# A two-layer kernel whose second layer takes its 256-token plain block first, between the last slots of layer one, with a scheduler that looks ahead

## The chip, the cores and the metric

The kernel runs on one core of one Trainium2 chip. The metric is the device time of one execution in microseconds (us). Each version is run several times; the median is compared.

## The reference

Windowed attention over q, k, v of 4 x 8 heads x 576 positions x 64 (half of the heads with a plain window of 32, half with a window of 32 at a stride of 4) gives x, 2304 tokens by 512. Two MLP layers follow:

```python
x = attention(q, k, v)              # 2304 x 512, float32
h = x @ moe_w_in                    # 512 x 2048
x = maximum(0.01 * h, h) @ moe_w_out
h = x @ moe2_w_in
out = (maximum(h, 0) + log1p(exp(-abs(h)))) @ moe2_w_out
```

All is float32. Matrix products take each operand as a high part in the matmul's own format and a low remainder, and add three products (high x high, high x low, low x high).

## The kernel before, in words

No order is written by hand. Every piece of work is an `Op` with an engine, a planned cost, dependencies, buffers that it takes (`acq`) and gives back (`rel`), and a due time (`target`, less `margin`). `run_schedule` (L109) plans all engines forward in time: an engine that is free takes the ready op with the earliest due time. The result is a list, and the instructions are emitted in that order; on the chip each engine then runs its own list strictly in order and waits where an operand isn't there. TensorE's list is fixed for the two layers by `chain`: each op of it is ordered behind the one before.

**Layer one** works in slots (`order`, L730). A slot is one block of tokens (256 to 352, mostly 288) with one of 16 pieces `f` of the hidden width. `g1` (L754, matmuls L747) makes a hidden tile in a PSUM bank `h`; ScalarE applies the leaky unit (`g1_leaky`, L763) and takes the high part (`g1_hi`, L768), VectorE the low part (`g1_lo`, L772); two slots later (`LAG`) `g2` (matmuls L790) adds it into the four banks `yp` of the block. After a block's last slot the four banks go through `y_evac` (ScalarE for e = 0 and 2, L798, VectorE for e = 1 and 3, L800) into `ys` (three buffers in SBUF), and `y_store` (L803) writes them to DRAM; a `ys` buffer is free again when its store has landed. The banks are then used by the next block, or, after the last block, by layer two. Attention for later blocks (scores L594, PV L674) and the conversion of the second layer's weights lie between the slots. The conversion loads a raw piece, and ScalarE's `rebias` (L282) is its first step; `C2A` and `C2B` set when pieces are due.

**Layer two** takes 2304 tokens as four blocks of 512 and one of 256 (`TL2`). For a block of 512, step m = (block c, pair of hidden pieces i) makes seven products of a 2 x 2 block scheme (`prod`, L924) of combined weights A11, A12, A22, S1 to S4 with combined inputs (`t_sum`, `t_hi`, `t_lo`), which VectorE adds into two units of 128 x 512. A unit passes |h|, exp, ln, 1+ (ScalarE, L959 to L970), three VectorE steps (L973 to L982), the high part on ScalarE (`hi`, L987) and the low part on VectorE (`lo`, L991); its |h| to `lo` holds one of the same three `ys` buffers. Then `g4` (L1014) multiplies it, in chunks of three matmuls, with `w_out` into four banks `yo`; at a block's end `o_evac` (L1022, L1024) copies each bank in two halves into one of five `o` buffers and `o_store` writes it out. `PATTERN` gives the order of products (digits) and chunks (a, b) in a step. The block of 256 tokens comes last: `plain` (L1002) makes its hidden tile `hp` directly, with A11, A12, A21, A22, and A21 is loaded late (`a21_load`) into S2's room. The second layer's weights (`comb_load`, L825; split by `comb_hi` L829 and `comb_lo` L833) use the rooms of layer one's weights as its last block frees them.

The change touches `run_schedule`, `comb_load` and its companions, `load_y`, `x_last`, `prod`'s numbering, `plain`, `o_store`, the constants, `pe`, `x_ready`, `product` and the loop that writes layer two's chain.

Of the kernel before, what the change touches and what calls it, by code (L numbers as in the profile page):

```python
# [11 lines left out]
F32 = mybir.dt.float32  # L12
# [14 lines left out]
def kernel(  # L27
# [80 lines left out]
    def run_schedule(slots):  # L108
# [53 lines left out]

        result = []
# [4 lines left out]
        while True:  # L168
# [14 lines left out]
            for e in engines:  # L183
# [10 lines left out]
                if e == "pe" and not opened and not best.optional and now - ready_at[best] < 0.3:  # L194

                    for o in pools[e]:
                        if o.optional and ready_at[o] <= now + 1e-9 and all(free[a] >= o.acq.count(a) for a in o.acq):
# [3 lines left out]
                            break  # L201
                pools[e].remove(best)
                for a in best.acq:
                    free[a] -= 1
# [14 lines left out]
                heapq.heappush(events, best.end)  # L219
                for u in best.next:  # L220
                    done(u, best.end if u.eng == e else now)
# [27 lines left out]
    class Piece:  # L249
# [52 lines left out]
        def sums(self, k):  # L302

            a = self.ct.bitcast(F32).rearrange("p (a n) -> p a n", a=4)
            if k == 0:
                self.cs = wraw.tile([P, 4, 2 * P], F32, tag="cp", name="cs", bufs=1)
            s = self.cs
            x, y, op = ((a[:, 2], a[:, 3], ALU.add), (s[:, 0], a[:, 0], ALU.subtract),
                        (a[:, 0], a[:, 2], ALU.subtract), (a[:, 1], s[:, 1], ALU.subtract))[k]
            nc.vector.tensor_tensor(out=s[:, k], in0=x, in1=y, op=op)  # L310
# [504 lines left out]
    def comb_load(i, half, j):  # L815
        if j == 0:
            comb[i, half] = wpool.tile([P, 4, 2, 2 * P], F32R, tag=f"w{2 * i + half}", name="w2")
            for n, nm in enumerate((("A11", "A12", "A22", "S1"), ("S2", "S3", "S4"))[half]):
                comb[i, nm] = comb[i, half][:, n]
            if half:  # L820
                spare[i] = comb[i, 1][:, 3].rearrange("p t n -> p (t n)")
        t = comb[i, half].bitcast(F32)
        dst, src = (((t[:, 0:2, 1], w2_a[i][:, 0:2]), (t[:, 2, 1], w2_a[i][:, 3]), (t[:, 3, 1], w2_s[i][:, 0])),
                    ((t[:, 0:3, 1], w2_s[i][:, 1:4]),))[half][j]
        nc.sync.dma_start(out=dst, in_=src)  # L825

    def comb_hi(i, half, j):
        t = comb[i, half][:, 2 * j:min(2 * j + 2, 4 - half)]
        nc.scalar.activation(out=t[:, :, 0], in_=t[:, :, 1].bitcast(F32), func=AF.Copy)  # L829

    def comb_lo(i, half, j):
        t = comb[i, half][:, 2 * j:min(2 * j + 2, 4 - half)]
        nc.vector.tensor_sub(out=t[:, :, 1], in0=t[:, :, 1].bitcast(F32), in1=t[:, :, 0].bitcast(F32))  # L833

    def a21_load(i):
        comb[i, "A21"] = comb[i, "S2"]
        nc.sync.dma_start(out=comb[i, "A21"][:, 1].bitcast(F32), in_=w2_a[i][:, 2])

    def a21_hi(i):
        t = comb[i, "A21"]  # L840
# [685 lines left out]
```

## Time and profile before

| | us |
|---|---|
| three runs | 925.34, 927.38, 930.04; median 927.38 |
| the profiled execution | 924.97 |
| its span, first to last instruction | 923.2 |
| TensorE (PE) busy | 886.5 (96%) |
| VectorE (DVE) busy | 707.4 (77%) |
| ScalarE (ACT) busy | 508.0 (55%) |
| GpSimd (POOL) busy | 136.7 (15%) |
| mean granted TensorE clock | 0.989 |

Layer one's matmuls fill the span to about 530 us, layer two's the rest; its block of 256 tokens runs from 865 us. An engine's idle time is told with what ended it. TensorE's number of matmuls is the same in both versions, so its idle time and its time at a granted clock below 1.00 are the parts to look at.

### The profile page before, as it was taken

To read this page: it belongs to the slowest core of one execution; us is meant where nothing else is said; L and a number is where in the kernel's file an instruction comes from. 1 tells how busy PE (TensorE), PEld (TensorE's weight loads), DVE (VectorE), ACT (ScalarE), POOL (GpSimd) and SP (SyncE) were. 2 spreads that over 40 slices of the span, in tenths; PEclk is the share of its full clock that TensorE was granted. 3 is DMA by queue.
4 is the path that set the end of the run, shared out by engine and by line. 5 is a ranking of instruction groups with operands and counts; after the bars stand their busy time and mean duration, and the time that the engine had idled before them with its cause. 6 is when DMAs were issued, how large, how long until landed. Compare 5 with 4: busy or idle time off the path is not lost.

```text
span 923.2 us, 16583 instructions
## 1 busy us (share of the span) xinstructions
PE 886.5 (96%) x6375; PEld 827.2 (90%) x6376; DVE 707.4 (77%) x1265; ACT 508.0 (55%) x983; POOL 136.7 (15%) x73
## 2 busy tenths in 40 slices
PE   6889999999999999999999979999999999999998
PEld 4779999999999999999999968888888888888887
DVE  3989994376796997978966777797778778777745
ACT  3768853334344434444456655675575666656554
POOL 4500030010352452423600000000000000000000
PEclk9979999999999999999999979999999999999999
DMA  8878122254555455554347823244335323533274
GB/s 228 212 226 293 21 43 48 75 139 141 166 127 182 109 145 162 157 148 126 125 154 228 311 88 92 92 142 151 104 107 171 103 93 122 169 118 113 98 224 164
DMA packets 157331, 131.90 MB, mean 143 GB/s; under 512 B 102340, under 2 KB 138180, under 8 KB 157124
## 3 DMA queue, kind: packets, MB, share of 16 engines
q1 hardware_dynamic: 154852, 130.26, 47.3%
q8 instruction: 50, 0.82, 0.4%
q10 hardware_dynamic: 2400, 0.59, 0.3%
q14 instruction: 29, 0.24, 0.1%
HBM read 104.60 MB, written 26.21 MB: 142 GB/s over the span
## 4 chain that ended last, share of the span: by engine, by line
PE 68%; DVE 14%; DMA 7%; ACT 3%; issue 2%; POOL 2%; SPq 1%; DVEq 0%; ACTq 0%; POOLq 0%
PE yo L1014 19%; PE h L747 15%; PE yp L790 15%; PE h L924 14%; PE hp L1002 2%; POOL sm L682 2%; DMA out_dram<-o 2%; DMA raw<-in_moe_w_out_dram 2%; PE sc L594 2%; DVE cf L300 2%; DMA yr<-y 1%; PE pv L643 1%; DMA y<-ys 1%; DVE xn L690 1%; SPq L487 1%
## 5 line engine op out<-in xcount | busy, mean ns | idle before, releaser
L1014 PE MATMUL yo<-wo,w 128*128 128x512 f32 x864 | 228.4, 399 | 10.6 <-ACT w L987 6.1
L747 PE MATMUL h<-xh,w 128*128 128x288 f32 (+2 forms) x1024 | 231.5, 301 | 1.2 <-DVE w L342 1.1
L790 PE MATMUL yp<-gh,w 128*128 128x288 f32 (+2 forms) x1024 | 229.2, 299 | 3.1 <-ACT ys L798 1.8
L1014 PEld LDWEIGHTS yo<-wo,w 128*128 128x128 f32 x864 | 153.2, 190 | 41.7 <-ACT w L987 6.5
L924 PEld LDWEIGHTS h<-tr,w 128*128 128x128 f32 x1344 | 175.0, 188 | 10.9
L924 PE MATMUL h<-tr,w 128*128 128x256 f32 x1344 | 177.4, 280 | 0.0
L790 PEld LDWEIGHTS yp<-gh,w 128*128 128x128 f32 x1024 | 171.6, 188 | 4.8 <-DVE ys L800 2.2
L747 PEld LDWEIGHTS h<-xh,w 128*128 128x128 f32 x1024 | 172.9, 190 | 2.8 <-DVE w L342 1.6
L747 PE MATMUL h<-xl,w 128*128 128x288 f32 (+2 forms) x512 | 152.1, 297 | 0.3 <-DVE xl L725 0.3
L790 PE MATMUL yp<-gl,w 128*128 128x288 f32 (+2 forms) x512 | 150.9, 295 | 0.0
L763 ACT ACTIVATE hc<-h 128x288 f32<-128x288 f32 (+2 forms) x128 | 52.1, 407 | 111.2 <-PE h L747 106.3
L747 PEld LDWEIGHTS h<-xl,w 128*128 128x128 f32 x512 | 97.3, 190 | 0.5 <-DVE xl L725 0.5
L790 PEld LDWEIGHTS yp<-gl,w 128*128 128x128 f32 x512 | 96.2, 188 | 0.4 <-DVE gl L772 0.3
L987 ACT ACTIVATE w<-ex 128x512 fp32r<-128x512 f32 (+1 forms) x73 | 45.4, 622 | 86.8 <-DVE ex L982 86.6
L618 POOL PARTITION_ALL_REDUCE mx<-s x24 | 50.2, 2090 | 265.6 <-DVE s L608 242.0
L772 DVE TENSOR_TENSOR gl<-hc,gh 128x288 fp32r<-128x288 f32 (+2 forms) x128 | 66.5, 521 | 26.5 <-ACT gh L768 25.9
L973 DVE SCALAR_TENSOR_TENSOR ln<-z,ln 128x512 f32<-128x512 f32 (+1 forms) x73 | 49.8, 683 | 40.8 <-ACT z L970 40.8
L282 ACT ACTIVATE cf<-raw 128x512 f32<-128x512 f32 (+1 forms) x48 | 39.9, 830 | 50.7 <-DMA raw<-in_moe_w_in_dram 26.5
L682 POOL PARTITION_ALL_REDUCE sm<-s x16 | 61.0, 3815 | 37.9 <-ACT s L625 37.9
L768 ACT ACTIVATE gh<-hc 128x288 fp32r<-128x288 f32 (+2 forms) x128 | 56.8, 444 | 3.1 <-ACT w L829 0.2
L991 DVE TENSOR_TENSOR w<-ex,w 128x512 fp32r<-128x512 f32 (+1 forms) x73 | 49.6, 679 | 9.6 <-ACT w L987 9.5
L300 DVE CUSTOM_DVE_ANT_0 cf<-raw,cf 128x1024 uint16<-128x1024 uint16 (+1 forms) x48 | 53.5, 1115 | 1.4
(108 smaller groups left out, 1164.7 us busy)
## 6 DMA issues: line engine op xcount, KB each, us to landing
wo<-w2o SPq DMA_DIRECT2D x80, 512.0 KB
raw<-in_moe_w_in_dram SPq DMA_DIRECT2D x32, 512.0 KB
raw<-in_moe_w_out_dram SPq DMA_DIRECT2D x32, 512.0 KB
w2o<-cf SPq DMA_DIRECT2D x16, 512.0 KB
out_dram<-o SPq DMA_DIRECT2D x36, 128.0 KB
w2a<-cf SPq DMA_DIRECT2D x8, 512.0 KB
w2s<-cs SPq DMA_DIRECT2D x8, 512.0 KB
qr<-in_q_dram SPq DMA_DIRECT2D x96, 36.0 KB
```

What stands on the lines that cost most here:

```text
L300: nc.vector.tensor_tensor(out=self.cf, in0=self.cf, in1=self.raw[:, :, 0], op=ALU.add)
L618: nc.gpsimd.partition_all_reduce(self.mx, self.sf, channels=P, reduce_op=bass_isa.ReduceOp.max)
L682: nc.gpsimd.partition_all_reduce(self.sm, self.sf, channels=P, reduce_op=bass_isa.ReduceOp.add)
L747: nc.tensor.matmul(out=h, lhsT=a[:, c, :], rhs=b_[:, c, :], start=(c == 0 and a is whi and b_ is xh), stop=(c == NC - 1 and a is wlo))
L763: nc.scalar.activation(out=hc, in_=hbank.pop(s), func=AF.Prelu, alpha=0.01)
L768: nc.scalar.activation(out=gh, in_=hcopy[s], func=AF.Copy)
L772: eng.tensor_sub(out=gl, in0=hcopy.pop(s), in1=gparts[s][0].bitcast(F32))
L790: nc.tensor.matmul(out=ybank[e][:, o:o + n], lhsT=a[:, e * P:(e + 1) * P], rhs=b_, start=(f == 0 and n == unit_len[u] and a is whi and b_ ...
L924: nc.tensor.matmul(out=bank[m, b][:, half], lhsT=w[:, a, kb * P:(kb + 1) * P], rhs=t[:, b_, kb], start=(kb == 0 and a + b_ == 0), stop=(kb ...
L973: nc.vector.scalar_tensor_tensor(out=self.ln, in0=self.z, scalar=1.0, in1=self.ln, op0=ALU.subtract, op1=ALU.subtract)
L991: nc.vector.tensor_sub(out=self.gl, in0=self.ex, in1=self.gh.bitcast(F32))
L1014: nc.tensor.matmul(out=obank[c, t], lhsT=a, rhs=b_, start=(opens and n == 0), stop=(closes and n == 2))
```

## The change

- The block of 256 tokens becomes block c = 0 of layer two. Its first hidden tile is made before layer one's last three `g2`, its second before the last one; the other six follow, with the chunks of the tile before the last between their halves. The blocks of 512 come after it.
- The weights A11, A12, A21, A22 are loaded by one transfer, S1, S3, S4 by another; S2 is loaded into A21's room when the block's tile i is done (before: three transfers and one, with A21 loaded late). A product waits only for the parts that it reads.
- In the last two steps of layer two other patterns (`LAST`) put the chunks behind the seventh product; the chain now ends with chunks of units 128 x 512.
- The planner, from 480 us of its own time, leaves ScalarE or VectorE free when an op that is more urgent by `GAP` comes within `AHEAD`.
- `y_evac` is due 5 us earlier (margin 8 for 3); second-layer weights are converted some 27 us earlier (`C2A`); attention's matmuls are planned 1 us later behind their operands (`SLACKT`).

```diff
+        coming = {e: [] for e in engines}
+        unbegun = {o: len(o.deps) + len(o.order) for o in ops}
+        due = {o: o.earliest for o in ops}
...
+                if e in ("dve", "act") and now > AHEAD_FROM:
+
+                    soon = [u for u in coming[e] if now + 1e-9 < due[u] <= now + min(AHEAD, best.cost)
+                            and u.prio < best.prio - GAP and all(free[a] >= u.acq.count(a) for a in u.acq)]
+                    if soon:
+                        heapq.heappush(events, min(due[u] for u in soon))
+                        continue
...
+        n = 4 - half
+        nc.sync.dma_start(out=t[:, 0:n, 1].bitcast(F32), in_=(w2_s if half else w2_a)[i][:, 0:n])
+
+    def comb_last(i):
+        comb[i, "S2"] = comb[i, "A21"]
+        nc.sync.dma_start(out=comb[i, "S2"][:, 1].bitcast(F32), in_=w2_s[i][:, 3])
...
+    def first_token(c):
+        return TL2 + (c - 1) * TP if c else 0
...
+    LAST = ('01aa23a4a56bbbb', '0123456aaaabbbb')
...
-    SLACKT = 2.0
+    SLACKT = 3.0
+    AHEAD_FROM, AHEAD, GAP = 480.0, 0.9, 2.0
...
-    C2A, C2B = 157.0, 19.9
+    C2A, C2B = 130.0, 20.0
...
-                            order=evs[-1:], acq=["ys"], margin=MG, target=tau(s + LAG + 1) + SLOT1 / 2)
+                            order=evs[-1:], acq=["ys"], margin=8.0, target=tau(s + LAG + 1) + SLOT1 / 2)
...
-        chain.append((NS1 - 2 if n < 4 else NS1 if n < 11 else NS1 + 1, 2 + 1e-4 * n, o))
+        chain.append((NS1 - 1 if n < 2 else NS1 if n < 4 else NS1 + 1, (0.5 if n < 2 else 2) + 1e-4 * n, o))
...
+    x_ready(0)
+    for j in range(NF2):
+        out_loads(0, (2 * j, 2 * j + 1))
+        g = plain_chunks(j - 2) if j >= 2 else ()
+        g = iter(g)
+        tag = "h" if j % 2 else "at"
+        for half in range(2):
+            o = Op("pe", 2 * GA, plain, j, half, deps=[opened, wready2[j, half], t_done[0]],
+                   acq=[tag] if half == 0 else [], rel=["t0", "t1"] if half and j == NF2 - 1 else [], target=clock[0])
+            pe(o)
+            if half:
+                unit_ops(("p", j), j, TP, lambda j=j: bank["p", j], [o], [tag])
+                comb_ops(j, 4, Op("dma", 0.4, comb_last, j, deps=[o], margin=MR))
+            for _ in range(2 if j >= 2 else 0):
+                pe(next(g))
...
+        for step in FIRST if m_ == 1 else LAST[m_ - NM] if m_ >= NM - len(LAST) else PATTERN:
+            pe(next(g_a if step == "a" else g_b) if step in "ab" else product(m_, int(step)))
...
+    for key in ((NM - 2, 1), (NM - 1, 0), (NM - 1, 1)):
+        for o in chunks(key):
+            pe(o)
```

How the emitted order moves at the places that matter. Line numbers of the changed kernel are its own: L1023 is `plain`, L1035 `g4`, L812 `g2`, L820 ScalarE's `y_evac`, L980 to L1008 a unit's steps on ScalarE, L917 `t_hi`, L304 `rebias`, L785 and L790 the leaky step and the high part.

TensorE before, from layer one's last `g2` (yp_6072 is its fourth bank) over the last products ahead of the first chunk of layer two:

```order
L790 MATMUL yp_6072<-gl,w 128x288
L790 MATMUL yp_6072<-gh,w 128x288
L924 MATMUL h_6776<-tr,w_6170 128x256 x6
L924 MATMUL h_6789<-tr,w_6212 128x256 x6
L924 MATMUL h_6789<-tr,w_6170 128x256 x6
L1014 MATMUL yo<-wo,w_6132 128x512 x2
L1014 MATMUL yo<-wo,w_6212 128x512
```

TensorE of the change, from the same `g2` (yp_6114 is its fourth bank) to the first chunk:

```order
L812 MATMUL yp_6114<-gh,w 128x288
L812 MATMUL yp_6114<-gl,w 128x288
L812 MATMUL yp_6114<-gh,w 128x288
L1023 MATMUL hp<-tr,w_6301 128x256 x12
L1035 MATMUL yo<-wo,w_6169 128x512 x2
L1035 MATMUL yo<-wo,w_6260 128x512
```

The first chunk now belongs to the plain block's tile 0, whose 24 matmuls stand three `g2` (36 matmuls) and tile 1 (24 matmuls) further up; before it belonged to step 0's first unit, with 42 products between that unit's last product and the chunk.

ScalarE before, around layer one's last evacuations (yp_6055 is bank 0, yp_6068 bank 2; L829 splits weights):

```order
L966 ACTIVATE ln<-ex 128x512
L970 ACTIVATE z<-ex 128x512
L798 ACTIVATE ys<-yp_6055 128x288
L966 ACTIVATE ln<-ex 128x512
L829 ACTIVATE w_6671<-w_6671 128x2x256
L970 ACTIVATE z<-ex 128x512
L829 ACTIVATE w_6671<-w_6671 128x256
L798 ACTIVATE ys<-yp_6068 128x288
L829 ACTIVATE w_6721<-w_6721 128x2x256
L987 ACTIVATE w_6132<-ex 128x512
```

ScalarE of the change at the same place (yp_6096 is bank 0, yp_6110 bank 2; L1008 is the high part of the plain block's first unit):

```order
L917 ACTIVATE tr<-yr 128x512 x2
L1008 ACTIVATE w_6169<-ex 128x512
L820 ACTIVATE ys<-yp_6096 128x288
L980 ACTIVATE ex<-hp 128x512
L820 ACTIVATE ys<-yp_6110 128x288
L983 ACTIVATE ex<-ex 128x512
L987 ACTIVATE ln<-ex 128x512
L991 ACTIVATE z<-ex 128x512
```

The first unit's high part, which stood behind both evacuations and three weight splits, now stands ahead of both. Two units stood in their steps around the evacuations before; now one is through and the second starts between them.

ScalarE before, at the block boundary near 414 us (yp_4539 is bank 0, yp_4551 bank 2):

```order
L763 ACTIVATE hc<-h 128x288
L768 ACTIVATE gh<-hc 128x288
L282 ACTIVATE cf<-raw 128x512
L798 ACTIVATE ys<-yp_4539 128x288
L763 ACTIVATE hc<-h 128x288
L798 ACTIVATE ys<-yp_4551 128x288
L768 ACTIVATE gh<-hc 128x288
```

ScalarE of the change at the same boundary (yp_4576, yp_4588):

```order
L785 ACTIVATE hc<-h 128x288
L820 ACTIVATE ys<-yp_4576 128x288
L790 ACTIVATE gh<-hc 128x288
L820 ACTIVATE ys<-yp_4588 128x288
L785 ACTIVATE hc<-h 128x288
L790 ACTIVATE gh<-hc 128x288
L304 ACTIVATE cf<-raw 128x512
```

The `rebias` that stood right ahead of the evacuation now stands behind it.

## Rows read from the trace of the kernel before

**Rows 1.** The page's first part: engine, busy us, share of the span, instructions.

```profile
PE 886.5 (96%) x6375; PEld 827.2 (90%) x6376; DVE 707.4 (77%) x1265; ACT 508.0 (55%) x983; POOL 136.7 (15%) x73
```

**Rows 2.** Busy us by stage: window, length, PE, PEld, DVE, ACT, POOL, PEclk, DMA.

```profile
250.00:515.00 265.00, 258.59 (x2033) 252.12 (x2032) 218.50 (x402) 124.41 (x265) 87.62 (x30) 1.00 0.52 156
515.00:546.00 31.00, 24.82 (x165) 22.89 (x164) 23.01 (x44) 20.79 (x45) 0.00 (x0) 0.83 0.53 172
546.00:865.00 319.00, 315.26 (x1970) 280.31 (x1969) 253.31 (x447) 200.38 (x372) 0.00 (x0) 1.00 0.38 121
865.00:912.00 47.00, 46.34 (x293) 41.16 (x293) 24.00 (x38) 25.15 (x47) 0.00 (x0) 1.00 0.61 180
```

**Rows 3.** The timeline of PE, 537 to 549 us; idle before in brackets.

```profile
537.56 1.22 PE L1014 MATMUL yo<-wo,w 128*128 128x512 f32 x2 [5.48 <-ACT w L987]
539.49 4.63 PE L1014 MATMUL yo<-wo,w 128*128 128x512 f32 x10 [0.70 <-DVE w L991]
543.92 1.99 PE L924 MATMUL h<-tr,w 128*128 128x256 f32 x12
545.74 1.55 PE L1014 MATMUL yo<-wo,w 128*128 128x512 f32 x6
547.13 1.56 PE L924 MATMUL h<-tr,w 128*128 128x256 f32 x12
548.53 1.56 PE L1014 MATMUL yo<-wo,w 128*128 128x512 f32 x6
```

**Rows 4.** The chain that ended last, 530 to 539 us: start, us, what.

```profile
530.85 2.75 DMA y<-ys
...
534.21 1.75 DMA y<-ys
```

**Rows 5.** Windows around a later wait and after this one, columns as in rows 2.

```profile
624.00:634.00 10.00, 8.61 (x56) 7.42 (x55) 7.73 (x15) 5.89 (x12) 0.00 (x0) 1.00 0.54 169
...
537.50:546.00 8.50, 7.74 (x26) 6.01 (x27) 6.21 (x11) 5.17 (x12) 0.00 (x0) 0.57 0.09 29
```

**Rows 6.** The timeline of ACT, one unit of the plain block: its first step.

```profile
897.35 0.58 ACT L959 ACTIVATE ex<-hp 128x512 f32<-128x512 f32 x1
```

**Rows 7.** The timeline of DVE, the same unit: its last step.

```profile
902.73 0.69 DVE L991 TENSOR_TENSOR w<-ex,w 128x512 fp32r<-128x512 f32 x1 [0.70 <-ACT w L987]
```

**Rows 8.** The timeline of ACT: a late A21's split, waiting for its load.

```profile
805.98 0.42 ACT L841 ACTIVATE w<-w 128x256 fp32r<-128x256 f32 x1 [0.36 <-DMA w<-w2a]
```

**Rows 9.** The timeline of SP, the same load's issue.

```profile
803.43 0.33 SPq L837 DMA_DIRECT2D w<-w2a  x1
```

**Rows 10.** The timeline of PE: waits of layer two at block ends and in the plain block.

```profile
628.72 1.67 PE L1014 MATMUL yo<-wo,w 128*128 128x512 f32 x6 [1.39 <-DVE o L1022]
...
800.30 1.70 PE L1014 MATMUL yo<-wo,w 128*128 128x512 f32 x6 [1.07 <-ACT o L1024]
...
892.24 1.92 PE L1014 MATMUL yo<-wo,w 128*128 128x512 f32 x6 [0.66 <-ACT w L987]
```

**Rows 11.** Who waited for whom on PE: us in total, times, longest; all of layer one.

```profile
PE yp L790 <- ACT ys L798: 1.8, 2, 1.3
PE pv L674 <- ACT s L625: 1.6, 3, 0.8
PE sc L594 <- DVE xn L702: 1.3, 1, 1.3
PE yp L790 <- DVE ys L800: 1.2, 3, 0.5
```

**Rows 12.** The timeline of ACT at the block boundary near 414 us.

```profile
413.82 0.66 ACT L282 ACTIVATE cf<-raw 128x512 f32<-128x512 f32 x1 [5.71 <-DMA raw<-in_moe_w_out_dram]
```

**Rows 13.** The timeline of PE, the same boundary.

```profile
414.83 0.40 PE L790 MATMUL yp<-gh,w 128*128 128x288 f32 x1 [1.25 <-ACT ys L798]
```

**Rows 14.** Who waited on ACT, 150 to 515 us: us in total, times, longest.

```profile
ACT cf L282 <- DMA raw<-in_moe_w_out_dram: 20.4, 8, 5.7
```

**Rows 15.** The timeline of SP at the end: the last stores of the output.

```profile
919.11 1.80 SPq L1027 DMA_DIRECT2D out_dram<-o  x4
```

More of the change, by code (lines that the diff above doesn't have):

```diff
@@ L201, in run_schedule @@
                             break
+                if e in ("dve", "act") and now > AHEAD_FROM:
[4 more added lines that the diff above has]
+                        continue
                 pools[e].remove(best)
+                if best in coming[e]:
+                    coming[e].remove(best)
                 for a in best.acq:
@@ L219, in run_schedule @@
                 heapq.heappush(events, best.end)
+                for u in best.users:
+                    begins(u, best.end + lag(best, u))
                 for u in best.next:
+                    begins(u, best.end if u.eng == e else now)
                     done(u, best.end if u.eng == e else now)
@@ L1027, in o_store @@
         nc.sync.dma_start(
-            out=out[c * TP + t * P:c * TP + (t + 1) * P, half * HT:(half + 1) * HT], in_=osb[c, t, half])
+            out=out[first_token(c) + t * P:first_token(c) + (t + 1) * P, half * HT:(half + 1) * HT], in_=osb[c, t, half])
     NS1 = len(order)
@@ L1404, in product @@
     def product(m, k_):
-        c, i = divmod(m, NF2)
-        half = 1 if k_ in (1, 3, 5) else 0
-        deps = [opened, *wready2[i, half], t_done[c, k_]]
+        c, i = m // NF2 + 1, m % NF2
+        parts = ((0, 1), (4,), (2,), (2,), (0,), (3,), (1,))[k_]
+        deps = [*(wready2[i, j] for j in parts), t_done[c, k_]]
         acq = [("h", "at", "h", "at")[(0, 2, 4, 5).index(k_)]] if k_ in (0, 2, 4, 5) else []
-        rel = [f"t{(7 * c + k_) % NTR}"] if i == NF2 - 1 else []
+        rel = [f"t{t_index(c, k_) % NTR}"] if i == NF2 - 1 else []
         o = prods[m, k_] = Op("pe", GA, prod, m, k_, deps=deps, acq=acq, rel=rel, target=clock[0])
@@ L1433 @@
         out_loads(c, (2 * i, 2 * i + 1))
-        g_a = chunks((m_ - 2, 1)) if m_ >= 2 else None
-        g_b = chunks((m_ - 1, 0)) if m_ >= 1 else None
-        for step in PATTERN if m_ != 1 else FIRST:
-            if step in "ab":
-                g = g_a if step == "a" else g_b
-                if g is not None:
-                    o = next(g)
-                    pe(o)
-            else:
-                pe(product(m_, int(step)))
-        for g in (g_a, g_b):
-            if g is not None:
-                assert next(g, None) is None
@@ new lines @@
+        g_a = chunks((m_ - 2, 1)) if m_ >= 2 else plain_chunks(NF2 - 2) if m_ == 0 else iter(())
+        g_b = chunks((m_ - 1, 0)) if m_ >= 1 else plain_chunks(NF2 - 1)
+        for step in FIRST if m_ == 1 else LAST[m_ - NM] if m_ >= NM - len(LAST) else PATTERN:
+            pe(next(g_a if step == "a" else g_b) if step in "ab" else product(m_, int(step)))
+        assert next(g_a, None) is None and next(g_b, None) is None
+    for key in ((NM - 2, 1), (NM - 1, 0), (NM - 1, 1)):
+        for o in chunks(key):
+            pe(o)
```

152 lines of the change are left out of this document (55 added, 97 removed).

## The prediction

> **What bounds the kernel now.** I read the page first. TensorE is busy 96% of the span [rows 1], and the change leaves its matmuls as they are, 12 per 128 x 256 product half and 3 per chunk. So nothing can be won or lost but TensorE's gaps and its clock. The table by stage comes next [rows 2], each row read as length less PE busy, with the granted clock beside it. From 250 to 515 us, layer one with attention, 6.4 of 265 us are idle at clock 1.00. From 515 to 546 us, where layer one hands over to layer two, 6.2 of 31 us are idle and the clock is 0.83. From 546 to 865 us, the blocks of 512, 3.7 of 319 us are idle; in the plain block behind them 0.7 of 47 us. The handover is the worst stretch by far.
>
> Then the handover itself. TensorE has run out of products when its first chunk waits 5.48 us for ScalarE's high part of a unit, and the next 0.70 us for VectorE's low part [rows 3]. ScalarE isn't slow there. The chain that ended last runs through three transfers of an evacuated bank to DRAM, one after the other, each ending where the next evacuation starts; the first took 2.75 us, the others 1.75 us [rows 4]. There are three `ys` buffers. The two units of step 0 hold two, so layer one's four last evacuations go through one, and each waits for the store of the one before. ScalarE and VectorE run in order, so the units' own steps wait behind those evacuations. The clock then falls: 0.57 from 537.5 to 546 us [rows 5], which is mostly the lower level.
>
> **The change, part by part.**
>
> *Handover.* The idle part is 5.48 + 0.70 = 6.18 us [rows 3]. The clock's part: at full clock six matmuls of 512 columns take 547.13 - 545.74 = 1.39 us and twelve of 256 take 548.53 - 547.13 = 1.40 us. After the wait, two of 512 took 538.79 - 537.56 = 1.23 us (539.49 less 0.70 gives the end) where 0.46 is due, ten took 543.92 - 539.49 = 4.43 us where 2.32 is due, and twelve of 256 took 545.74 - 543.92 = 1.82 us [rows 3]. That is 0.77 + 2.11 + 0.42 = 3.3 us. Together 9.5 us are there to win.
>
> In the change the plain block's tile 0 is made before the last three `g2`. Until its first chunk TensorE has those three `g2`, tile 1 and half of tile 2. A `g2` is 12 matmuls of 288 columns, nearly those of one 1.4 us half tile and an eighth more, so 1.6 us; the sum is 3 x 1.6 + 2.8 + 1.4 = 9.0 us. A unit of that block took 903.4 - 897.4 = 6.0 us from the first step to the end of the last [rows 6, 7], undisturbed. Bank 0 is complete two `g2`, tile 1 and a quarter `g2` after tile 0, 3.2 + 2.8 + 0.4 = 6.4 us. So unit 0 is just done before the evacuations and has returned its buffer; two evacuations find room at once. The third and fourth wait for a store, about 2.7 us behind an evacuation that took place less than half a microsecond earlier [rows 4]. Unit 1 has its |h| step between them on ScalarE, so its chain is late by some 2.3 us: 2.3 + 6.0 = 8.3 us after bank 0. TensorE needs it after three more quarter `g2`, three half tiles and two pairs of chunks, 1.2 + 4.2 + 2.8 = 8.2 us. It is a close race; with weight splits between, I take 0.7 us of wait. Its bounds are 0 and the old 9.5 us. **Net -8.8 us.** Such a short wait should leave the clock alone: a wait of 1.39 us [rows 10] stands in a window at 1.00 [rows 5], and only the long one is followed by a lower clock. The Trainium skill ("TensorE: Matmul & The Clock Gate", the section on psum-queue depth-cycling) says that short idles between groups of matmuls, where PSUM banks are used in turn, can make the clock swing to its lower level again and again. The trace disagrees: the plain block alternates half tiles and chunks in this way at 1.00 [rows 2]. By the row the short wait costs itself alone.
>
> *The plain block at its new place.* Eight units at 5.6 us each: VectorE had 24.0 of 47 us busy there [rows 2], so the eleven input sums and low parts for the next block and the weight splits have room. New beside it is the load of S2 when a tile is done, with its split on ScalarE ahead of that unit's high part. Before, the same sort of load was issued at 803.43 and ended a wait of 0.36 us at 805.98 [rows 8, 9], so it lands in 2.5 us; the first four of a unit's nine steps take about as long (4/9 of 6.0 is 2.7 us), and the high part must wait for three VectorE steps anyway. Chunks follow their tile by two pairs of chunks and three half tiles or more, 8.4 us, against the unit's 6.0. I cost this at 0; should that cover fail by 1 us per tile it is 8 us (a rival). Its old wait of 0.66 us [rows 10] was in the tail plain block, behind four banks' evacuations of the block before; that goes: **-0.7 us**.
>
> *Block ends.* The block's four banks need eight half copies with five buffers, so stores are waited for: 1.39 and 1.07 us at two of the three ends that are followed by another block of 512 [rows 10]. `PATTERN` is unchanged there and three such ends remain. The plain block's end opens only four half copies, for which five buffers do. **0 us**; the look-ahead could win one or two.
>
> *Layer one.* TensorE's waits there are 1.8 + 1.2 us for evacuations and 1.6 + 1.3 us for attention [rows 11]. At 414 us ScalarE waited 5.71 us for a raw weight piece [rows 12] with the evacuation behind it, and TensorE then waited 1.25 us for that evacuation [rows 13]. At none of the last four boundaries inside layer one does the new order put a raw piece right ahead of the evacuations. But the pieces must still be waited for somewhere: 8 waits for output pieces alone sum to 20.4 us [rows 14], and most cost TensorE nothing, because two hidden banks and the lag of two slots cover them. I take off 1.5 of the 3.0 us, and 1.0 of 2.9 us for planning attention a microsecond later: **-2.5 us**, bounds -6 (all gone) and +4 (as much again as the evacuations and one attention wait).
>
> *The end.* Before, the last chunks closed two banks and four stores were issued in 1.80 us, 0.45 us each [rows 15]. Now four banks close in the last 2.1 us, 0.7 us apart. Eight issues take 3.6 us for 1.8 us, and begin 1.4 us earlier against the last close: **+0.4 us**; with eight stores under way at once up to +2. Twenty chunks (14 us) follow the last product, twice a unit's 6.0 us, so units aren't late there.
>
> *Nothing:* fewer and larger weight loads (they are issued before the handover), and the earlier start of conversion as such; its price, if there is one, is that of the raw pieces above.
>
> Sum: -8.8 - 0.7 - 2.5 + 0.4 = **-11.6 us**. The profiled execution took 924.97 us, so 913.4 us. The median of the runs is 2.4 us above the profiled one; I add that, and predict **916.0 us**, 1.2% less than 927.38. A measurement of this kernel can tell about 0.5%, 4.6 us, from no change.
>
> **The rivals.**
>
> *The handover waits again.* For: three buffers still serve four evacuations and two units. If unit 0 is late by a few microseconds, the second evacuation waits too, two store times of 2.75 and 1.75 us come ahead of unit 1, TensorE stands 3.5 us and the clock falls once more (3.3 us): 6.8 us in place of 0.7, so 922 us. Against: the 9.0 us for a 6.0 us unit.
>
> *The plain block's units are late.* S2's load blocks ScalarE, 1 us for each of eight tiles: 924 us. Against: the 8.4 us.
>
> *Slower.* Conversion waits. A raw piece that comes 5.7 us late costs TensorE about 1.3 us [rows 12, 13]. There are 32 such pieces. If the earlier dates push each load up against attention's loads on SP's queue so that 12 more wait so long, layer one loses 16 us and the whole is near 932 us. It decides from 9 on (11.6 / 1.3). Against: the 7 other waits behind the 20.4 us [rows 14] sum to 14.7 us, and cost TensorE at most the 1.75 us of evacuation waits left beside that 1.25 us [rows 11].
>
> *The clock swings.* If each wait of about 1 us were followed by a lower clock as the long one was, the handover and three block ends would each cost 3.3 us more: 916 + 13 = 929 us. Against: the window at 1.00 around the wait of 1.39 us [rows 5, 10]. (The Trainium skill's rule on short idles, above, would make it come out so.)
>
> *More is won.* Layer one's waits all go: 912 us or less.
>
> **How the numbers follow.** The forecast (911.5 to 920) has 0.66; more 0.09; the handover again 0.10; late units 0.08; slower 0.05; the swinging clock 0.02. The range 911 to 923.5 leaves out the slower cases, half of the late units and the best of "more". Faster by over 0.5% means below 922.7: the forecast, "more" and most of the handover case, 0.83; within 0.5% 0.12; slower 0.05.
>
> **What would show it.** Right: no PE wait over 1.5 us between 510 and 560 us, PEclk 1.00 in that stretch, the plain block's `hp` matmuls at about 515 to 565 us in near-gapless pairs, three waits of 1 us at block ends, less than 5 us of PE waits in 250 to 510 us. Wrong: chunks waiting for `w` with a DMA of `ys` in the chain; ScalarE waiting for `w2s` in the plain block; waits of `h` or `yp` behind raw pieces adding up to 8 us or more.

## The result: slower by 0.6%, and the profile after

The changed kernel took 933.95 us (median of 17 runs, 930.16 to 941.27), the kernel before 928.46 us (17 runs on the same chips, 925.34 to 931.05). The ratio is 1.0061, with a 95% interval of 1.0041 to 1.0081. The forecast was 916.0 us, the range 911.0 to 923.5 us, so both the time and the sign are wrong. The profiled execution took 933.49 us; its span is 931.7 us, 8.5 us more than before.

The page's first part stands against [rows 1]: TensorE's busy time is the same within 0.3 us, so on balance the loss is in its gaps.

```profile
PE 886.2 (95%) x6376; PEld 827.7 (89%) x6376; DVE 718.5 (77%) x1261; ACT 507.9 (55%) x978; POOL 134.9 (14%) x73
```

The handover, as busy time by stage with the columns of [rows 2], shows no gap and the full clock, where [rows 2] have 24.82 us busy at 0.83:

```profile
515.00:546.00 31.00, 31.00 (x242) 31.00 (x241) 20.07 (x37) 18.70 (x39) 0.00 (x0) 1.00 0.53 166
```

Layer one, in the same columns, from 100 to 520 us, in the kernel before:

```profile
100.00:520.00 420.00, 413.58 (x3228) 406.33 (x3227) 325.18 (x610) 195.16 (x402) 109.23 (x39) 1.00 0.48 137
```

The same in the change, and two pieces of it:

```profile
100.00:520.00 420.00, 400.95 (x3078) 392.17 (x3077) 321.55 (x586) 184.56 (x380) 107.47 (x39) 0.99 0.48 134
...
340.00:370.00 30.00, 23.45 (x169) 22.46 (x168) 18.27 (x36) 10.32 (x24) 5.90 (x2) 0.94 0.45 135
...
460.00:490.00 30.00, 27.19 (x208) 26.03 (x207) 24.03 (x42) 12.90 (x28) 9.86 (x4) 0.94 0.29 95
```

So 19.05 us are idle where 6.42 were. Who waited for whom on TensorE (us in all, times, longest) names the places that [rows 11] name, with other numbers: evacuations by VectorE cost 8.0 us for 1.2, and two groups stand here that [rows 11] don't have, low parts (`gl`) and the high parts of a block's tokens (`xh`).

```profile
PE yp L812 <- DVE ys L822: 8.0, 3, 4.6
PE yo L1035 <- ACT o L1045: 5.3, 3, 3.0
...
PE yp L812 <- DVE gl L794: 3.3, 2, 1.6
PE h L769 <- ACT xh L743: 3.2, 2, 2.0
PE sc L616 <- DVE xn L724: 2.9, 4, 1.1
```

The worst wait stands at the block boundary near 357 us. From SP's timeline, then VectorE's, ScalarE's and TensorE's (start, us, instruction; idle before in brackets):

```profile
356.00 0.34 SPq L353 DMA_DIRECT2D w2o<-cf  x1
356.39 0.44 SPq L288 DMA_DIRECT2D raw<-in_moe_w_in_dram  x1
357.26 5.73 SPq L825 DMA_DIRECT2D y<-ys  x4
```

```profile
356.26 0.45 DVE L822 COPY ys<-yp 128x288 f32<-128x288 f32 x1
362.18 0.46 DVE L822 COPY ys<-yp 128x288 f32<-128x288 f32 x1 [5.10 <-DMA y<-ys]
```

```profile
361.66 0.66 ACT L304 ACTIVATE cf<-raw 128x512 f32<-128x512 f32 x1 [4.35 <-DMA raw<-in_moe_w_in_dram]
```

```profile
362.69 0.61 PE L812 MATMUL yp<-gh,w 128*128 128x288 f32 x1 [4.63 <-DVE ys L822]
```

The chain that ended last goes through the same store:

```profile
357.26 4.83 DMA y<-ys
...
362.18 0.47 DVE ys L822
```

With the new dates SP issues a store and a load of the conversion, 512 KB each, just ahead of the block's four `y<-ys` stores. The first of these lands 4.83 us after its issue, where [rows 4] show 1.75 to 2.75 us. Three `ys` buffers serve four banks, so VectorE's second evacuation waits for that landing, and TensorE for the evacuation. In the kernel before the last load ahead of the same stores was issued 5.5 us earlier, and the same evacuation waited 0.56 us (SP's timeline, then VectorE's):

```profile
347.79 0.42 SPq L270 DMA_DIRECT2D raw<-in_moe_w_out_dram  x1
353.25 2.66 SPq L803 DMA_DIRECT2D y<-ys  x4
```

```profile
355.11 0.46 DVE L800 COPY ys<-yp 128x288 f32<-128x288 f32 x1 [0.56 <-DMA y<-ys]
```

In the change it is the same as at 357 us, with smaller waits, at 423 us (VectorE 4.29 us, TensorE 2.08) and at 229 us (3.50 and 1.24).

### The profile page after: what moved, and what is told of

It is laid out like the page before. It is cut to its first block, busy times and chain, and to the rows that moved or that the text cites. A ratio compares the mean times of both kernels' runs of the same rounds, so it can differ in the third digit from the quotient of the medians.

```text
span 931.7 us, 16557 instructions
## 1 busy us (share of the span) xinstructions
PE 886.2 (95%) x6376; PEld 827.7 (89%) x6376; DVE 718.5 (77%) x1261; ACT 507.9 (55%) x978; POOL 134.9 (14%) x73
## 4 chain that ended last, share of the span: by engine, by line
PE 69%; DVE 15%; DMA 5%; issue 3%; ACT 3%; SPq 1%; DVEq 0%; ACTq 0%
PE yo L1035 19%; PE h L945 15%; PE h L769 15%; PE yp L812 15%; PE hp L1023 2%; PE sc L616 2%; DMA out_dram<-o 2%; DMA y<-ys 2%; DVE cf L322 1%; DVE gl L794 1%; DVE cp L309 1%; DVE xn L712 1%; PE pv L665 1%; DVE rd L717 1%; DVE cs L332 1%
## 5 line engine op out<-in xcount | busy, mean ns | idle before, releaser
L812 PE MATMUL yp<-gh,w 128*128 128x288 f32 (+2 forms) x1024 | 231.8, 301 | 8.0 <-DVE ys L822 8.0
L1035 PE MATMUL yo<-wo,w 128*128 128x512 f32 x864 | 224.4, 395 | 5.4 <-ACT o L1045 5.3
L1035 PEld LDWEIGHTS yo<-wo,w 128*128 128x128 f32 x864 | 152.1, 188 | 34.6 <-ACT o L1045 6.6
L812 PEld LDWEIGHTS yp<-gh,w 128*128 128x128 f32 x1024 | 173.1, 190 | 9.8 <-DVE ys L822 8.7
L812 PE MATMUL yp<-gl,w 128*128 128x288 f32 (+2 forms) x512 | 152.0, 297 | 3.3 <-DVE gl L794 3.3
L785 ACT ACTIVATE hc<-h 128x288 f32<-128x288 f32 (+2 forms) x128 | 52.0, 406 | 127.4 <-PE h L769 122.4
L812 PEld LDWEIGHTS yp<-gl,w 128*128 128x128 f32 x512 | 97.1, 190 | 3.9 <-DVE gl L794 3.7
L794 DVE TENSOR_TENSOR gl<-hc,gh 128x288 fp32r<-128x288 f32 (+2 forms) x128 | 72.4, 566 | 27.3 <-ACT gh L790 25.9
L1008 ACT ACTIVATE w<-ex 128x512 fp32r<-128x512 f32 x72 | 45.2, 628 | 71.1 <-DVE ex L1003 71.0
L1012 DVE TENSOR_TENSOR w<-ex,w 128x512 fp32r<-128x512 f32 x72 | 49.8, 691 | 35.0 <-ACT w L1008 34.2
L994 DVE SCALAR_TENSOR_TENSOR ln<-z,ln 128x512 f32<-128x512 f32 x72 | 49.6, 688 | 23.3 <-ACT z L991 23.1
L704 POOL PARTITION_ALL_REDUCE sm<-s x16 | 59.0, 3690 | 38.5 <-ACT s L647 38.5
L790 ACT ACTIVATE gh<-hc 128x288 fp32r<-128x288 f32 (+2 forms) x128 | 56.7, 443 | 2.7
L304 ACT ACTIVATE cf<-raw 128x512 f32<-128x512 f32 (+1 forms) x48 | 39.9, 830 | 30.7 <-DMA raw<-in_moe_w_in_dram 16.1
L309 DVE TENSOR_SCALAR cp<-cf 128x512 uint32<-128x512 uint32 (+1 forms) x48 | 37.5, 782 | 17.3 <-ACT cf L304 10.9
```

What stands on the lines that cost most here:

```text
L309: nc.vector.tensor_single_scalar(out=self.cp, in_=self.cf, scalar=3, op=ALU.logical_shift_left)
L704: nc.gpsimd.partition_all_reduce(self.sm, self.sf, channels=P, reduce_op=bass_isa.ReduceOp.add)
L785: nc.scalar.activation(out=hc, in_=hbank.pop(s), func=AF.Prelu, alpha=0.01)
L790: nc.scalar.activation(out=gh, in_=hcopy[s], func=AF.Copy)
L794: eng.tensor_sub(out=gl, in0=hcopy.pop(s), in1=gparts[s][0].bitcast(F32))
L812: nc.tensor.matmul(out=ybank[e][:, o:o + n], lhsT=a[:, e * P:(e + 1) * P], rhs=b_, start=(f == 0 and n == unit_len[u] and a is whi and b_ ...
```

## Experiments

Times are medians; a ratio is to the kernel before on the same chip.

| kernel | us | ratio, 95% interval |
|---|---|---|
| change, old dates (`dates_back`) | 917.22 | 0.9902, 0.9884 to 0.9920 |
| change, old margin (`margin_back`) | 931.04 | 1.0038, 1.0016 to 1.0060 |
| change, old slack (`slack_back`) | 930.19 | 1.0042, 1.0018 to 1.0067 |
| before, new dates (`before_dates`) | 933.49 | 1.0080, 1.0055 to 1.0105 |
| change, old dates and slack (`dates_slack_back`) | 920.33 | 0.9924, 0.9905 to 0.9943 |
| change, old dates, no look-ahead (`dates_back_no_ahead`) | 923.90 | 0.9964, 0.9948 to 0.9980 |
| change, transfers behind the stores (`behind`) | 938.10 | 1.0131, 1.0093 to 1.0168 |
| change, dates 137 / 19.9 (`c137`) | 921.93 | 0.9942, 0.9922 to 0.9961 |
| change, dates 150 / 20 (`c150`) | 927.86 | 1.0025, 0.9996 to 1.0054 |
| change, dates 153 / 20 (`c153`) | 932.05 | 1.0061, 1.0041 to 1.0080 |
| change, dates 160 / 20 (`c160`) | 931.63 | 1.0052, 1.0033 to 1.0071 |
| change, old dates, added store (`dose`) | 923.14 | 0.9952, 0.9933 to 0.9970 |
| change, loads start 3 us earlier (`lead25`) | 916.24 | 0.9892, 0.9867 to 0.9917 |
| change, loads start 2 us earlier (`lead24`) | 928.33 | 1.0018, 1.0000 to 1.0037 |

### Which part of the change loses the time

Three parts act on layer one; each was undone alone, and the dates were also put into the kernel before.

```diff
-    C2A, C2B = 130.0, 20.0
+    C2A, C2B = 157.0, 19.9
```

> The change with one line undone: the second-layer weights are due on the old dates (C2A, C2B = 157, 19.9). Theory of the dates: the new dates put a 512 KB store of converted weights and a 512 KB raw load on the queue 1 to 3 us ahead of a block's four stores of ys; those then land 4 to 5 us after issue, VectorE's fourth evacuation waits for the first store, and TensorE waits 1.2 + 4.6 + 2.1 us. With the old dates the yp waits fall from 8.0 to 3 us or less, the evacuations wait at most 1.5 us each for a store, layer one wins some 9 us with the clock, and the time is 920 to 925 us, under the kernel before. Rival, the earlier rank of the evacuations (margin 8): the waits stay near 8 us and the time near 933. Rival, attention planned later (SLACKT 3): yp waits stay, time near 933.

917.22 us, 3 us below the range of the theory. TensorE's waits for VectorE's evacuations fall to 0.9 us, VectorE's for `y` stores from 18.2 to 11.9, and from 250 to 560 us the clock is 1.00. One part of the expectation failed: at 414 us an evacuation still waits 3.12 us for a store, where 1.5 at most was expected.

```diff
-                            order=evs[-1:], acq=["ys"], margin=8.0, target=tau(s + LAG + 1) + SLOT1 / 2)
+                            order=evs[-1:], acq=["ys"], margin=MG, target=tau(s + LAG + 1) + SLOT1 / 2)
```

> The change with the evacuations' margin back from 8 to its old value, the rest kept. Theory of the dates: what the queue carries ahead of the stores of ys is the same, so the waits of yp stay at 6 to 10 us and the time at 930 to 937 us. Rival, the rank of the evacuations: the waits fall under 4 us, the time to 921 to 926.

931.04 us, with 6.9 us of TensorE's waits for VectorE's evacuations and 19.5 us of VectorE's for `y` stores: the waits hardly move.

```diff
-    SLACKT = 3.0
+    SLACKT = 2.0
```

> The change with SLACKT back from 3 to 2, the rest kept. Theory of the dates: yp waits stay within 6 to 10 us, though at one boundary the raw load is issued ahead of the store of weights; attention's waits (xh, sc, pv, xl: 7 us) may move by 2 us either way; time 929 to 936 us. Rival, attention planned later is the cause: time 921 to 926.

930.19 us; evacuations still cost TensorE 10.2 us.

```diff
-    C2A, C2B = 157.0, 19.9
+    C2A, C2B = 130.0, 20.0
```

> The kernel before with the new dates alone (C2A, C2B = 130, 20), block of 256 still last. Theory of the dates: layer one loses what the change lost there, 6 to 13 us, and the handover keeps its stall of 6 us and the lower clock; the time is 934 to 942 us. Rival, the new dates harm only together with the other edits: 924 to 931 us.

This edit is to the kernel before: 933.49 us, with 11.0 us of waits for evacuations, so the dates lose time without the rest of the change too. It is 0.5 us below the expected range; the wait at the handover, expected to stay at 6 us, is 3.82 us here. The dates are the part. With the old ones the median lies in the range that was forecast, but not because every term came true: layer one idles 7.23 us from 100 to 520 us, 0.8 more than before where 2.5 less was forecast, and the profiled execution took 916.89 us where the sum gave 913.4.

### What the other parts are worth with the old dates

> The change with the old dates and the old place of attention's matmuls. If planning attention 1 us later is worth something inside layer one, this is slower than the 917.2 us of the change with the old dates alone, 918 to 921 us, with 1 to 3 us more of waits for pv and sc; if it is worth nothing there and only its order at block ends counts (3.4 us of waits where the change had 5.3), 914 to 917 us.

920.33 us, 2 us by the ratio (0.9924 against 0.9902, intervals that overlap), which is the time of the first case without its reason: the waits for `pv` and `sc` hardly grow, and from 100 to 520 us TensorE idles 7.48 us for 7.23. The traces differ more at the last block end: behind a wait of 2.76 us the clock is 0.64 from 840.2 to 845 us, some 1.7 us (4.8 x 0.36), where the run with the old dates alone stayed at full clock behind 2.90 us. So it isn't shown that the later attention is worth anything.

```diff
-    AHEAD_FROM, AHEAD, GAP = 480.0, 0.9, 2.0
+    AHEAD_FROM, AHEAD, GAP = 9480.0, 0.9, 2.0
```

> The change with the old dates and without the planner's look-ahead. If the plain block's place alone closes the handover, TensorE waits no more than 2 us between 500 and 560 us and the time is 916 to 919 us. Rival (the look-ahead is what keeps ScalarE and VectorE free for the first units): waits of 3 to 7 us there, some of them followed by a lower clock, 921 to 927 us.

923.90 us, the rival's time without its waits: the idle time from 500 to 560 us is 2.6 us for 1.1, where 3 to 7 us were expected, and no lower clock follows it. More is lost at the last block end, which TensorE leaves after a wait of 2.43 us at a lower clock, six matmuls in 3.27 us ([rows 10] have 1.67 for six at full clock); with the look-ahead the wait there was longer and the clock stayed full, three in 0.96 us. Without the look-ahead, and then with it:

```profile
840.18 3.27 PE L1035 MATMUL yo<-wo,w 128*128 128x512 f32 x6 [2.43 <-DVE o L1043]
```

```profile
838.23 0.96 PE L1035 MATMUL yo<-wo,w 128*128 128x512 f32 x3 [2.90 <-ACT o L1045]
```

So the run with the look-ahead is some 6 us faster here, but part of that is the clock at one place and not the look-ahead's planned work.

### Is it the transfers ahead of the stores?

The conversion's transfers that the plan has within 6 us ahead of a block's first `y` store were moved behind its fourth, in the finished list (the condition that no user of them lies in between is left out here):

```diff
+    for first, *_, last in stores:
+        late = [o for o in schedule[max(0, first - 60):first]
+                if o.eng == "dma" and o.start > schedule[first].start - 6.0
...
+        schedule[i0:last + 1] = [o for o in schedule[i0:last + 1] if o not in late] + late
```

> The change with its new dates kept, but the conversion's transfers (w2o stores, raw loads) that are planned within 6 us ahead of a block's first y store are issued behind its fourth. Theory (the y stores land late because two 512 KB transfers are issued right ahead of them): at the boundaries of 362 and 428 us both transfers move, so TensorE's waits for VectorE's evacuations of 4.6 and 2.1 us go there, VectorE waits under 9 us for y stores in all, and the time is 918 to 925 us. Rival (the conversion's earlier place as such crowds the engines, whatever the order at the boundaries): TensorE still waits 7 us or more for evacuations, 930 to 936 us.

At the boundaries of 357 and 423 us the stores behaved as the theory said, and the time did not: 938.10 us. (At the boundary of 229 us, 231 in this run, the raw load stays ahead of the stores, and VectorE waits 3.58 us there; its waits for `y` stores are 11.4 us in all, where the theory gave under 9.) The boundary of 357 us, from SP's, VectorE's and ScalarE's timelines:

```profile
358.03 2.72 SPq L825 DMA_DIRECT2D y<-ys  x4
360.81 0.42 SPq L353 DMA_DIRECT2D w2o<-cf  x1
361.28 0.45 SPq L288 DMA_DIRECT2D raw<-in_moe_w_in_dram  x1
```

```profile
359.95 0.46 DVE L822 COPY ys<-yp 128x288 f32<-128x288 f32 x1 [1.05 <-DMA y<-ys]
```

```profile
366.30 0.66 ACT L304 ACTIVATE cf<-raw 128x512 f32<-128x512 f32 x1 [6.78 <-DMA raw<-in_moe_w_in_dram]
```

The evacuation now waits 1.05 us for 5.10. But the raw piece, issued 5 us later, is late on ScalarE by 6.78 us. Twelve us later TensorE waits 3.40 us in attention, with a lower clock behind it (0.58 from 380 to 386 us); that this comes from the late piece isn't shown, since the profile names no releaser for that wait. From 100 to 520 us 19.86 us are idle, 0.8 more than in the change. So at these dates stores in time alone give nothing back: other waits stand in their place.

### Earliness or where the transfers fall

The conversion has a cycle of 20 us, two raw pieces each. Dates a whole cycle earlier keep each piece's place against the block boundaries.

```diff
-    C2A, C2B = 130.0, 20.0
+    C2A, C2B = 137.0, 19.9
```

> The change with the conversion's dates 20 us earlier than the old ones (137.0, 19.9) and not 27 us earlier (130.0, 20.0): one whole cycle of 19.9 us, so the pieces stand to the block boundaries as with the old dates. Theory (only where the transfers fall against the y stores counts): like the change with the old dates, 915 to 921 us, waits for VectorE's evacuations under 2 us. Rival (earlier is worse in itself): 20 of 27 us of the loss of 16.7 us come back, 927 to 932 us.

> The change with the conversion's dates at 150.0 and 20.0: only 7 us earlier than the old ones, but exactly one cycle of 20 us later than the change's own, so that a w2o store and a raw load stand right ahead of the y stores again. Theory (where the transfers fall against the y stores counts, not how early conversion is): as slow as the change, 928 to 936 us, waits for VectorE's evacuations of 6 us or more. Rival (earliness costs, 16.7 us for 27 us): 7 us of it cost 4 to 5 us, 920 to 924 us.

> The change with the conversion's dates at 153.0 and 20.0, 4 us earlier than the old ones: at two of the four boundaries a w2o store and a raw load stand right ahead of the y stores, at one a w2o store, at one a raw load. Theory of where the transfers fall: between the two, 921 to 929 us, waits for VectorE's evacuations of 3 to 6 us. Rival (earliness): 918 to 921 us.

> The change with the conversion's dates at 160.0 and 20.0, 3 us later than the old ones; a raw load is the last transfer ahead of the y stores, and the w2o store and the next raw load stand behind them, as with the old dates. Theory of where the transfers fall: 915 to 920 us, waits for VectorE's evacuations under 2 us. If later dates push the last weights into the handover, waits of h or yo between 500 and 560 us and 920 to 925 us.

The others differ in the same line. 137 took 921.93 us: 20 us earlier keeps 12 of the 16.7 us, 0.9 us outside the theory's range, so earliness isn't what costs most. 150 took 927.86 us, just under the theory's range and over the rival's, with 4.1 us of waits for evacuations where the theory gave 6 or more (its profiled execution, 7 us over the median, began at a clock of 0.86 over the first 100 us). But 153 and 160 took 932.05 and 931.63 us, slower than any theory said. At 160, 3 us later than the old dates, a raw load stands some 5 us or more ahead of the stores at most boundaries, and 0.5 us at one. From SP and VectorE:

```profile
420.73 0.42 SPq L292 DMA_DIRECT2D raw<-in_moe_w_out_dram  x1
421.25 5.34 SPq L825 DMA_DIRECT2D y<-ys  x4
```

```profile
425.79 0.46 DVE L822 COPY ys<-yp 128x288 f32<-128x288 f32 x1 [4.74 <-DMA y<-ys]
```

That one cost TensorE 3.28 us; the other waits of that run (`sc` 4.9 us, `xh` 3.8) stand elsewhere. Boundaries of the runs side by side (each named by its run and the time of its first store) show what the wait of VectorE's second evacuation goes with:

| last raw load ahead of the first store | VectorE's wait, us |
|---|---|
| 0.5 us (change 423, `c150` 485, `c153` 294, `c160` 421) | 4.29, 4.50, 5.27, 4.74 |
| 0.9 us (change 357) | 5.10 |
| 1.9, 2.2, 2.4 us (`c153` 228, `c150` 299, change 229) | 3.08, 2.06, 3.50 |
| 3.5 us (change 293) | 1.09 |
| 3.7 us, and a store 2.2 us (`dates_back` 414) | 3.12 |
| only a store, 1.7 and 2.6 us ahead (`c153` 361, `lead25` 350) | 1.09, 1.10 |
| only a store, 0.4 and 0.8 us ahead (`slack_back` 487 and 357) | 2.83, 3.36 |
| a load of `wo`, 0.4 us ahead (`lead25` 471, `lead24` 488) | 3.53, 4.61 |

The second line from the end widens the theory: a store of 512 KB close ahead is enough. At 357 us of `slack_back`, where the last raw load was issued 8.8 us ahead, TensorE waited 3.02 us for this evacuation (SP, then VectorE):

```profile
356.28 0.33 SPq L353 DMA_DIRECT2D w2o<-cf  x1
357.04 4.11 SPq L825 DMA_DIRECT2D y<-ys  x4
```

```profile
360.35 0.46 DVE L822 COPY ys<-yp 128x288 f32<-128x288 f32 x1 [3.36 <-DMA y<-ys]
```

The Trainium skill ("DMA: Bandwidth & Descriptors", the section on queues, rings and completion order) says that what SP issues lies in one ring on each of the DMA engines, and that each engine takes its descriptors in the ring's order, though a later one may finish its write before an earlier one. The table agrees with that order as far as it goes (1.09 us behind a raw load 3.5 us ahead, 4.29 to 5.27 us behind one 0.5 us ahead); the rings themselves no run here shows.

### What a late store costs by itself

```diff
+        if e == 0 and u in (3, 4):
+            n = unit_len[u]
+            more = dram.tile([P, 4, n], F32, tag=f"more{u}", name=f"more{u}")
+            nc.sync.dma_start(out=more, in_=ysum[u, e].unsqueeze(1).to_broadcast([P, 4, n]))
         nc.sync.dma_start(out=y_d[u][:, e], in_=ysum[u, e])
```

> The change with the old dates (917.2 us), and at two block boundaries, near 352 and 414 us, one added transfer: it writes the first evacuated bank four times (590 KB) to a spare place in DRAM right ahead of that bank's y store, which both delays the store and holds its buffer. Nothing of the conversion moves. Theory (late y stores are what costs, 4.6 and 2.1 us of TensorE's waiting in the change and a lower clock behind them): VectorE waits 4 to 6 us there, TensorE 2 to 5 us at each, and the time is 924 to 930 us. Rival (the loss of 16.7 us came from where the conversion's steps fall among the other engines' work, and the late stores only stand where other waits would): under 920 us.

923.14 us, between the two again: 5.9 us more than with the old dates alone by the medians, 4.6 by the ratios (the lower edge of the theory was 924). The two boundaries, on VectorE and on TensorE:

```profile
356.32 0.46 DVE L822 COPY ys<-yp 128x288 f32<-128x288 f32 x1 [3.18 <-DMA y<-ys]
...
421.60 0.46 DVE L822 COPY ys<-yp 128x288 f32<-128x288 f32 x1 [4.66 <-DMA y<-ys]
```

```profile
356.83 0.40 PE L812 MATMUL yp<-gh,w 128*128 128x288 f32 x1 [1.18 <-DVE ys L822]
...
422.11 0.40 PE L812 MATMUL yp<-gh,w 128*128 128x288 f32 x1 [2.45 <-DVE ys L822]
```

About 2 us of VectorE's wait are covered, the rest is TensorE's. So late stores at two boundaries cost about a third of the 16.7 us by themselves; the dose is smaller than the change's own, 3.6 us of TensorE's waits for 8.0, and no lower clock followed here.

### The same dates, the loads earlier

```diff
-    T0, C2L = 35.0, 22.0
+    T0, C2L = 35.0, 25.0
```

> The change with its new dates for every step of the conversion, but each raw piece's load may start 3 us earlier (25.0 for 22.0); in the plan the loads near the block boundaries then stand 4 to 7 us ahead of the y stores, where the change has them 1.3 to 1.7 us ahead at the two worst. Theory (a raw load issued right ahead of the y stores is what costs, and moving it behind them only moved the wait to the piece): the waits of 4.6 and 2.1 us go and ScalarE waits for no piece there, VectorE waits under 9 us for y stores in all, 919 to 926 us. Rival (the new dates put conversion's steps on ScalarE and VectorE ahead of urgent ones, loads apart): still 929 us or more, with 10 us or more of other waits in layer one.

916.24 us, 3 us below the range of the theory: with the change's own dates and loads that may start 3 us earlier the loss is gone. The boundary near 350 us, on SP and on VectorE:

```profile
347.73 0.34 SPq L353 DMA_DIRECT2D w2o<-cf  x1
350.37 2.70 SPq L825 DMA_DIRECT2D y<-ys  x4
353.13 0.42 SPq L292 DMA_DIRECT2D raw<-in_moe_w_out_dram  x1
```

```profile
352.27 0.46 DVE L822 COPY ys<-yp 128x288 f32<-128x288 f32 x1 [1.10 <-DMA y<-ys]
```

No raw load stands close ahead, and the stores land in time. It is not so at every boundary: at 471 us a load of `wo` is issued 0.36 us ahead, VectorE waits 3.53 us and TensorE 1.31, and VectorE's waits for `y` stores are 11.5 us in all where under 9 were expected. From 100 to 520 us 7.16 us are idle, at clock 1.00:

```profile
100.00:520.00 420.00, 412.84 (x3218) 405.74 (x3217) 328.72 (x606) 196.35 (x403) 110.50 (x39) 1.00 0.49 140
```

> The same with 24.0 for 22.0, so 2 us earlier: in the plan 4 to 6 us ahead of the y stores. Theory: like the run with 25.0 within 3 us, 919 to 927 us; rival: 929 us or more.

With 24.0 it is 928.33 us: this expectation failed. At the boundaries of 366 and 428 us the stores are in time there too (1.10 and 1.42 us); at 488 us, with a load of `wo` 0.36 us ahead, TensorE waits 2.39 us for an evacuation. Another transfer is late as well. VectorE's first step of a piece waits for a store of sums that still holds its buffer, with the low part of a block's tokens two steps behind it; TensorE then waits 3.82 us for that (`xl`), near 359 us:

```profile
357.77 0.43 DVE L309 TENSOR_SCALAR cp<-cf 128x512 uint32<-128x512 uint32 x1 [3.59 <-DMA w2s<-cs]
358.12 0.45 DVE L794 TENSOR_TENSOR gl<-hc,gh 128x288 fp32r<-128x288 f32 x1
358.49 0.63 DVE L747 TENSOR_TENSOR xl<-xn,xh 128x288 fp32r<-128x288 f32 x1
```

The profiled execution of `lead24` also began at a clock of 0.85 over its first 100 us (0.97 in `lead25`), so not all of the 12 us between the two comes from these waits.

## Why the prediction was wrong

*Handover: right.* -9.5 us where -8.8 was forecast. There is no wait between 500 and 570 us, so not even the 0.7 us that were left for the close race (with the old dates one of 1.13 us stands there, so the race is as close as was said). The rivals of a second wait and of late units didn't occur, and the wait of the plain block [rows 10] is gone.

*Layer one and "nothing": the step that failed.* The prediction took 2.5 us off layer one, with bounds of -6 and +4, and put the earlier conversion under "Nothing", since "its price, if there is one, is that of the raw pieces above". It looked at ScalarE's order at the boundaries, where no raw piece stood ahead of the evacuations any more, and not at SP's, where a raw load had moved to just ahead of the `y` stores. With the old dates the change took 16.7 us less by the medians (14.7 by the ratios), so that is the price of the term put at nothing. Layer one came out 12.6 us worse in idle time. Its lower clock costs 4.8 us more in the profiled execution, as length times (1 - clock) of the three stretches behind waits of 4.63, 2.08 and 2.04 us (two rows each for the last two):

```profile
362.70:366.00 3.30, 3.30 (x14) 3.30 (x15) 2.14 (x5) 0.53 (x1) 0.00 (x0) 0.57 0.68 199
...
428.90:432.00 3.10, 3.10 (x17) 3.10 (x18) 2.87 (x6) 0.19 (x1) 0.00 (x0) 0.74 0.15 48
432.00:436.00 4.00, 4.00 (x25) 4.00 (x24) 2.44 (x5) 0.86 (x2) 1.96 (x1) 0.78 0.77 262
484.00:488.00 4.00, 3.69 (x16) 3.48 (x17) 3.29 (x7) 3.20 (x7) 0.00 (x0) 0.62 0.11 43
488.00:492.00 4.00, 4.00 (x30) 4.00 (x30) 1.51 (x3) 1.56 (x4) 0.00 (x0) 0.95 0.42 160
```

*The slower rival* had the right family, a raw transfer that is late for an in-order engine, and gave 932 us. That this is near the measured time is luck. It counted late pieces on ScalarE at 1.3 us each, but from 100 to 520 us ScalarE's waits for raw pieces fell, from 46.9 to 26.9 us. Late were the stores behind the loads, on whose buffers the evacuations depend.

*Block ends* cost 5.3 us for 3.4 before, +2 where 0 was forecast: the wait before the last block is 2.98 us. With the old `SLACKT` it was 1.30 us in one run (`slack_back`) and 2.76 in another (`dates_slack_back`), so what sets it stays open. *The end* came at +0.5 us for +0.4. The 916.0 us stands 0.2 above its own terms (913.4 + 2.4), which changes nothing.

*The sum.* -9.5 (handover) - 0.7 (old wait) + 12.6 + 4.8 (layer one) + 2.0 (block ends) + 0.5 (end) = +9.7 us; the first stores of layer one are issued at 158.63 us where they were at 160.29, which takes off 1.7. That is +8.0 of the 8.5 us by which the span grew.

*What is shown, and what isn't.* Against `lead25`, whose dates are the same, the change idles 11.9 us more in layer one and loses the 4.8 us of clock, 16.7 of the 17.4 us between the spans. Evacuations are 6.7 us of the idle time, and the clock behind two of them 3.1 us. The remaining idle 5.2 us are waits for `gl` (3.3 us, none in `lead25`) and `sc` (2.9 for 0.5), less a little elsewhere; those for `xh` are 3.2 us here and 4.0 in `lead25`. The remaining 1.7 us of clock stand behind a wait for `xh` of 2.04 us, where `lead25` has one of 2.52 us at full clock. For the two waits for `gl` the trace has a cause. While GpSimd reduces, a VectorE step takes 3.02 us that elsewhere takes 0.69, and a low part stands right behind it (on GpSimd, VectorE and TensorE); at 340 us the low part itself takes 2.79 us for 0.46 in the same way, and TensorE waits 1.62 us.

```profile
278.12 3.60 POOL L704 PARTITION_ALL_REDUCE sm<-s  x1 [2.39 <-ACT s L647]
```

```profile
278.18 3.02 DVE L313 SCALAR_TENSOR_TENSOR cf<-cf,cp 128x512 uint32<-128x512 uint32 x1
```

```profile
281.62 0.40 PE L812 MATMUL yp<-gl,w 128*128 128x288 f32 x1 [1.63 <-DVE gl L794]
```

Every version has 13 to 16 steps between 100 and 520 us that run over 1 us longer than others of their kind; what differs is which step is hit (low parts at seven places in the change, at two in `lead25`). Which of the other waits come from this, and which from late transfers, was not separated, since each edit of a date also makes the planner place other steps anew. So in the profiled execution some 10 of the 16.7 us are traced to late stores, by the waits and the clock behind them; the cause of the rest stays open, and `behind`, which put the stores of the two worst boundaries right without new dates, gave nothing back, with a raw piece late in their place. A fourth `ys` buffer, or stores issued from another engine's queue, the direct cures for the stores, weren't tried.

## What to carry to other kernels

When a change moves transfers, compare the order of the queue that issues them as well as that of the engines: here a small store whose buffer is waited for was late when it was issued within 2.4 us behind a 512 KB load, or within 0.8 us behind a 512 KB store. Eight settings of two dates and a lead in the same kernel lie between 916 and 934 us, so shifting a table of dates that was tuned for one order of work can't be priced at nothing; bound such a term by what the tightest buffer costs when its transfer is late. The version to keep is the change with loads that start 3 us earlier, or with the old dates: 1.1% and 1.0% faster than before. With loads 2 us earlier it is no faster than before, so such a setting holds for this kernel as it stands and is no rule.

## What the runs showed of the hardware

A store of one bank takes under 2 us from issue to the next use of its buffer when the last 512 KB transfer was issued 2.6 us ahead (350.37 to 352.27 us in `lead25`). Right behind a store and a load of 512 KB it takes 4.9 us (357.26 to 362.18 us in the change), and 0.8 us behind a 512 KB store alone 3.3 us (357.04 to 360.35 us in `slack_back`).

A VectorE step that runs while GpSimd reduces can take several times as long: 3.02 us for 0.69, 2.79 us for 0.46 (the change, at 278 and 340 us).

The length of a wait alone doesn't tell whether the lower clock follows. Behind 2.08 and 2.04 us the granted clock was 0.74 and 0.62, between its two levels (1.2 and 2.4 GHz). At the same places of `margin_back`, behind 2.03 and 2.01 us, it was 1.00; that run idles 18.37 us from 100 to 520 us for the change's 19.05, so most of the 4 us between the two spans is clock, behind waits that are alike. Behind 2.45 us (`dose`, at 422 us), 2.52 us (`lead25`, at 345 us) and 2.90 us (the change with the old dates, at 838 us) TensorE went on at full clock too.

The prediction weighed the Trainium skill's rule on short idles ("TensorE: Matmul & The Clock Gate", the section on psum-queue depth-cycling) against a wait of 1.39 us. The runs bear that rule out only in part: waits of 1.24 to 1.63 us stand in windows at 1.00 here too, while three of the change's waits from 2.04 us on were followed by a lower clock that cost 1.4 to 1.7 us each.
